# Key features of a batch in one block, its kv products in another, and the selector product in the kv bank

## Chip, cores, metric

One core of a Trainium2 chip. The metric is device time of one execution in microseconds (us). Every run quoted here is of the fast state; the granted TensorE clock (the share of full speed that the throttle left, as a mean of the run) was 0.985 to 1.000. Profiles are of single executions, and their span is some 2.2 us shorter than the time.

## The reference, cut to what matters

Attention with polynomial features, then a feed-forward layer with ELU; 4 batches, 4 heads, 1088 positions, head size 32, rank 8, hidden size 2048.

```python
def phi(x):                                    # 64 features of a row
    a = einsum('rd,bhsd->bhsr', S1, x); b = einsum('rd,bhsd->bhsr', S2, x)
    return einsum('bhsi,bhsj->bhsij', a, b).reshape(..., 64)
kv = einsum('bhsf,bhsd->bhfd', phi(k), v);  z = phi(k).sum(axis=2)
x  = (phi(q) @ kv) / (phi(q) @ z + 1e-6)       # then heads side by side: 4352 x 128
h  = x @ w_in
out = where(h > 0, h, exp(min(h, 0)) - 1) @ w_out
```

All of a batch's keys must have gone into `kv` and `z` before the batch's first query is finished.

## The kernel before

The dense part is a loop of 72 steps. A step multiplies 512 rows by two slices of `w_in` (tile `h`), applies the ELU on ScalarE (`e`: two activations per slice) and VectorE (`gg`), and two steps later adds the product with `w_out` to `o`. `o` has one buffer; when a group (or, for groups 0 and 1, a segment of one) ends, it is emptied into `oT` or `ob` before the next `o` product may start. The attention work of later batches and groups is hung into these steps, between `h` and `o`:

```python
for n in range(N + 4):
    if 2 <= n < N: mm1(g, cp)                     # h: two products of 512 columns
    for f, *a in extra.get(n, ()): f(*a)          # "at": side work, ahead of the ELU
    if 2 <= n < N: elu(g, cp)                     # e on ScalarE, gg on VectorE
    for f, *a in extra.get((n, 1), ()): f(*a)     # "late": after the ELU
    if 2 <= n < N + 2: mm2(...)                   # o of step n - 2; fin1 empties o
```

The side work of one batch, in the order of its data:

```python
KG = [range(0, 4), range(4, 8), range(8, KT)]    # 9 key tiles; the last has 64 rows
def KF(b, gi):                                   # key features: 8, 8 and 1 products
    abp = psum.tile([P, 512], F32, name="abp", tag="aux")     # tag aux: 2 buffers
    for j, i in enumerate(tiles):
        for u in range(rows // 64):
            nc.tensor.matmul(abp[64*u:64*u+64, j*64:j*64+64], kT[b][:, u*KT+i, :], Sab, tile_position=(0, 64*u))
    nc.scalar.copy(ab, abp)                      # ScalarE empties the bank
def KO(b, gi): ...                               # VectorE: kp = outer product of ab
def KA(b, gi): ...                               # kv += kp' v: 16, 16 and 4 products, 64-column tiles
def KC(b): ...                                   # ScalarE: kvz = copy of kv
def KZ1(b): ...                                  # GpSimd: zm = z times a mask
def KZ2(b):                                      # selector product, full width
    wps = psum.tile([P, 512], F32, name="wps", tag="aux")
    nc.tensor.matmul(wps[:, :H*R], SX, zm)
...
for b in range(1, B):
    n = NP * (b * NT // 8) - 12 + 2 * (b == 1)   # 6, 20, 36
    at(n, transp, kT, "k", b, 0, NT)             # VectorE, 1.3 us
    for i in range(3):
        at(n+1+i, KF, b, i); at(n+1+i, KO, b, i); at(n+2+i, KA, b, i)
    late(n+4, KC, b); late(n+4, KZ1, b); late(n+4, KS, b)
    at(n+5, KZ2, b); at(n+3, transp, qT, "q", b, 0, NT)
for g in range(2, NQ):                           # a group's queries
    n = NP * (g - 1) + (g == 2)
    at(n+3, q1, g); late(n+3, q2, g); at(n+5, q4, g); at(n+6, q5, g)
```

`q1` writes `abwp` (query features, 64-column tiles), `q4` writes `qtp` (transposes, full width), `q5` writes `xps` (32-column tiles). Products in float32 appear as two passes each in the trace, transposes as one.

## Time and profile before

| | before |
|---|---|
| time, median of 3 (range) | 303.12 us (302.90 to 303.38) |
| span of the profile | 300.9 us |
| TensorE, ScalarE, VectorE busy | 96%, 62%, 56% |
| dense block, start to start | 1.72 us |

A timeline line gives the start, the duration, the engine, the line of the program, the operation, the tiles (out<-in), the shape, how many passes were merged, and in brackets the idle time before it with what ended it. Durations of matmuls overlap, so what a block costs is the next block's start minus its own. The prediction below shows the lines.

### The profile page before, as it was taken

Reading aid. Unit: us, or ns where it says so; the run is one execution under the profiler, and the core shown is the slowest. Engines: PE = TensorE matmul, PEld = TensorE weight load, DVE = VectorE, ACT = ScalarE, POOL = GpSimd, SP = SyncE. Lnnn points to the kernel's source line nnn. Section 1 sums busy time; section 2 is a strip of 40 time slices with the busy share of each in tenths; the row PEclk is TensorE's granted clock in tenths of the full one; section 3 lists DMA queues with packets and bytes.
Section 4 is the critical chain, followed back from the end, with each engine's and each line's share of the span. In section 5 each row is a group of like instructions: output and inputs, shape, how many; then the busy total and the mean of one; then the engine's idle time right before and its main releaser. Section 6 shows DMA issues by size and latency. Waiting matters only on the chain.

```text
span 300.9 us, 4049 instructions
## 1 busy us (share of the span) xinstructions
PE 290.1 (96%) x1454; PEld 147.7 (49%) x1454; DVE 169.7 (56%) x297; ACT 187.8 (62%) x354; POOL 17.1 (6%) x45
## 2 busy tenths in 40 slices
PE   8987999999999999999999999999999999999994
PEld 5863344644444455444544464445444444444682
DVE  5788899963745565536344656426443644354441
ACT  1526896565666645746775656656774687568682
POOL 2010023440000000100000000100000000000000
PEclk9999999999999999999999999999999999999999
DMA  6932998320010100001001100001001000110020
GB/s 187 338 118 74 200 216 201 48 74 0 9 28 9 27 2 0 2 9 27 2 1 17 18 2 0 0 14 23 0 0 23 16 0 1 15 22 0 3 33 17
DMA packets 38291, 13.37 MB, mean 44 GB/s; under 512 B 32768, under 2 KB 36480, under 8 KB 38272
## 3 DMA queue, kind: packets, MB, share of 16 engines
q1 hardware_dynamic: 37984, 12.86, 19.0%
q10 hardware_dynamic: 288, 0.26, 0.3%
q8 instruction: 11, 0.18, 0.2%
q14 instruction: 8, 0.07, 0.1%
HBM read 10.88 MB, written 2.23 MB: 44 GB/s over the span
## 4 chain that ended last, share of the span: by engine, by line
PE 83%; DVE 8%; ACT 3%; DMA 2%; issue 2%; SPq 1%; DVEq 0%
PE o L522 36%; PE h L493 34%; PE xps L472 3%; PE kv L293 3%; PE qtp L457 2%; PE abwp L360 2%; DMA v<-in_v_dram 2%; DVE gg L508 1%; ACT e L502 1%; PE abp L266 1%; ACT e L501 1%; DVE kT L247 1%; DVE kp L253 1%; DVE W L114 1%; PE x0ps L424 1%
## 5 line engine op out<-in xcount | busy, mean ns | idle before, releaser
L508 DVE SCALAR_TENSOR_TENSOR gg<-e,h 128x512 f32<-128x512 f32 (+1 forms) x144 | 93.0, 654 | 98.3 <-ACT e L502 97.8
L522 PE MATMUL o<-gg,W 128*128 128x512 f32 (+1 forms) x288 | 131.1, 578 | 1.2 <-ACT oT L535 0.7
L493 PE MATMUL h<-xg,W 128*128 128x512 f32 (+1 forms) x288 | 128.8, 569 | 1.8 <-DVE xg L484 0.7
L501 ACT ACTIVATE e<-h 128x512 f32<-128x512 f32 (+1 forms) x144 | 81.4, 565 | 26.1 <-PE h L493 25.7
L502 ACT ACTIVATE e<-e 128x512 f32<-128x512 f32 (+1 forms) x144 | 87.3, 606 | 4.6
L493 PEld LDWEIGHTS h<-xg,W 128*128 128x128 f32 x288 | 54.5, 190 | 65.2 <-issue 55.2
L522 PEld LDWEIGHTS o<-gg,W 128*128 128x128 f32 x288 | 51.9, 190 | 51.4 <-issue 43.7
L270 ACT COPY ab<-abp 128x256 f32<-128x256 f32 (+1 forms) x12 | 3.7, 317 | 25.0 <-PE abp L266 25.0
L365 ACT COPY abw<-abwp 128x384 f32<-128x384 f32 (+1 forms) x8 | 3.7, 458 | 22.9 <-PE abwp L360 22.9
L253 DVE TENSOR_TENSOR kp<-ab 128x1024 f32<-128x1024 f32 (+1 forms) x12 | 12.2, 1022 | 8.4 <-ACT ab L270 8.2
L458 ACT COPY qpT<-qtp 128x512 f32<-128x512 f32 (+1 forms) x16 | 8.3, 561 | 12.6 <-PE qtp L457 12.6
L293 PEld LDWEIGHTS kv<-v,kp 128*64 128x64 f32 (+1 forms) x288 | 9.5, 139 | 7.5 <-DVE gg L508 5.3
L293 PE MATMUL kv<-v,kp 128*64 128x33 f32 (+3 forms) x288 | 10.8, 226 | 0.3 <-DMA v<-in_v_dram 0.3
L381 DVE TENSOR_TENSOR qp<-an,abw 128x1024 f32<-128x1024 f32 (+1 forms) x8 | 9.3, 1159 | 0.3
L472 PE MATMUL xps<-qpT,kvS 64*32 64x128 f32 (+2 forms) x200 | 8.7, 298 | 0.3 <-ACT qpT L458 0.3
L483 ACT COPY xg<-xps 128x256 f32<-128x256 f32 (+1 forms) x8 | 2.9, 359 | 9.8 <-PE xps L472 9.8
L457 PEld LDWEIGHTS qtp<-ident,qp 128*128 128x128 f32 x60 | 6.8, 140 | 4.4 <-issue 4.0
L457 PE MATMUL qtp<-ident,qp 128*128 128x128 f32 x60 | 8.2, 277 | 0.6 <-DVE qp L381 0.6
L313 POOL TENSOR_TENSOR zm<-kvz,zmask 128x32 f32<-128x32 f32 x3 | 0.7, 241 | 126.0 <-ACT kvz L307 126.0
L266 PE MATMUL abp<-Sab,kT 128*64 128x64 f32 x136 | 7.4, 249 | 0.5 <-DVE kT L247 0.5
L360 PEld LDWEIGHTS abwp<-SW,qT 128*64 128x64 f32 x120 | 5.2, 136 | 5.4 <-issue 5.3
L266 PEld LDWEIGHTS abp<-Sab,kT 128*64 128x64 f32 x136 | 6.1, 159 | 3.6 <-issue 2.9
(84 smaller groups left out, 126.2 us busy)
## 6 DMA issues: line engine op xcount, KB each, us to landing
raw<-in_moe_w_in_dram SPq DMA_DIRECT2D x8, 256.0 KB, 5.7
raw<-in_moe_w_out_dram SPq DMA_DIRECT2D x8, 256.0 KB, 6.6
out_dram<-ob SPq DMA_DIRECT2D x104, 16.0 KB, 1.5
hd_k<-in_k_dram SPq DMA_DIRECT2D x3, 544.0 KB, 5.3
hd_q<-in_q_dram SPq DMA_DIRECT2D x3, 544.0 KB, 3.8
v<-in_v_dram SPq DMA_DIRECT2D x12, 72.0 KB, 5.3
v<-in_v_dram SPq DMA_DIRECT2D x12, 64.0 KB, 3.4
hd_k<-in_k_dram SPq DMA_DIRECT2D x1, 288.0 KB, 3.4
```

Of the source, the lines that this page charges most:

```text
L253: nc.vector.tensor_mul(dst, _ap(a_, list(a_.ap[1:]) + [[0, R]]), _ap(b_, [b_.ap[1], [0, R], b_.ap[2]]))
L266: nc.tensor.matmul(abp[64 * u:64 * u + 64, j * 64:j * 64 + 64], kT[b][:, u * KT + i, :], Sab[:].rearrange("p h y -> p (h y)"), skip_group_ ...
L293: nc.tensor.matmul(kv[64 * hp:64 * hp + 64, g2, :n], kp[:rows, j, h].rearrange("p i j -> p (i j)"), _ap(vt[b][:rows, off:off + D], [[VN - ...
L360: nc.tensor.matmul(p[64 * u:64 * u + 64, i * 96:i * 96 + 96], qT[b][:, t, :], SW[:, b].rearrange("p h x r -> p (h x r)"), skip_group_check ...
L381: nc.vector.tensor_mul(qp[g][:, :m], _ap(a_, list(a_.ap[1:]) + [[0, R]]), _ap(b_, [b_.ap[1], [0, R], b_.ap[2]]))
L457: nc.tensor.transpose(p[:, o:o + P], qp[g][:, r:r + 2].rearrange("p t i j -> p (t i j)"), ident[:])
L472: nc.tensor.matmul(xp[w][D * h:D * h + D, :nh * P].rearrange("p (m s) -> p m s", s=P)[:, m0:m0 + m, s], kvS[64 * w:64 * w + 64, b, h, :], ...
L493: nc.tensor.matmul(hs[g, cp][c][:, :n], W[:, cp, c * P:c * P + P], xg[g][:, :n])
L501: nc.scalar.activation(e, hs[g, cp][c][:, :n], RELU, scale=-1.0)
L502: nc.scalar.activation(e, e, EXP, scale=-1.0)
L508: nc.vector.scalar_tensor_tensor(gs[g, cp][:, c, :n], es[g, cp][:, c, :n], -1.0, hs[g, cp][c][:, :n], op0=ADD, op1=MAX)
L522: nc.tensor.matmul(ops[g][:, :n], W[:, cp, (2 + c) * P:(3 + c) * P], gg[:, c, :n], start=(first and c == 0), stop=(last and c == 1))
```

## The change

The intent is to leave the full-width products (128x128 tiles) less often; one such departure to narrower tiles and back is called an excursion below. Key features of a batch stand in one block, the kv products in one block (for batches 2 and 3 next to a group's query features), and the selector product goes into spare columns of the kv bank, so that no third auxiliary buffer is needed near it. The last key product (tile 8, "product 17") shares the bank of the second four tiles.

```diff
     def KF(b, gi):
-        abp = psum.tile([P, 512], F32, name="abp", tag="aux")
+        if gi < 2:
+            abps[b] = psum.tile([P, 512], F32, name="abp", tag="aux")
+        abp = abps[b] if gi < 2 else abps[b][:, 256:]
...
-            kv_ps[b] = psum.tile([P, 2, 2 * D], F32, name="kv", tag="kv", bufs=1)
+            kv_ps[b] = psum.tile([P, 4, 2 * D], F32, name="kv", tag="kv", bufs=1)
...
-        wps = psum.tile([P, 512], F32, name="wps", tag="aux")
+        wps = kv_ps[b][:, 2]
...
-        n = NP * (b * NT // 8) - 12 + 2 * (b == 1)
-        at(n, transp, kT, "k", b, 0, NT)
+        n = NP - 2 if b == 1 else NP * (b * NT // 8 - 2) + 1          # 6, 17, 33
+        at(n - 1, transp, kT, "k", b, 0, NT)
         for i in range(3):
-            at(n + 1 + i, KF, b, i)
-            at(n + 1 + i, KO, b, i)
-            at(n + 2 + i, KA, b, i)
-        late(n + 4, KC, b)          # KZ1, KS alike
-        at(n + 5, KZ2, b)
+            at(n, KF, b, i)
+            at(n + (i > 0), KO, b, i)
+            at(n + 2, KA, b, i)
+        late(n + 2, KC, b)          # KZ1, KS alike
+        at(n + 4, KZ2, b)
```

More of the change, by code (lines that the diff above doesn't have):

```diff
@@ L256 @@
     kvS = const.tile([P, B, H, D], F32, name="kvS")
-    kv_ps, feats, zms, kvz = {}, {}, {}, {}
+    abps, kv_ps, feats, zms, kvz = {}, {}, {}, {}, {}
     def KF(b, gi):
-        abp = psum.tile([P, 512], F32, name="abp", tag="aux")
+        if gi < 2:
+            abps[b] = psum.tile([P, 512], F32, name="abp", tag="aux")
+        abp = abps[b] if gi < 2 else abps[b][:, 256:]
         tiles = KG[gi]
@@ L299, in KC @@
     def KC(b):
-        kv = kv_ps[b][:, :, :D + 1]
+        kv = kv_ps[b][:, :2, :D + 1]
         kvz[b] = work.tile([P, 2, 2, D + 1], F32, name="kvz", tag="kvz")
@@ L630 @@
     for b in range(1, B):
-        n = NP * (b * NT // 8) - 12 + 2 * (b == 1)
-        at(n, transp, kT, "k", b, 0, NT)
+        n = NP - 2 if b == 1 else NP * (b * NT // 8 - 2) + 1
+        at(n - 1, transp, kT, "k", b, 0, NT)
         for i in range(3):
-            at(n + 1 + i, KF, b, i)
-            at(n + 1 + i, KO, b, i)
-            at(n + 2 + i, KA, b, i)
-        late(n + 4, KC, b)
-        late(n + 4, KZ1, b)
-        late(n + 4, KS, b)
-        at(n + 5, KZ2, b)
+            at(n, KF, b, i)
+            at(n + (i > 0), KO, b, i)
+            at(n + 2, KA, b, i)
+        late(n + 2, KC, b)
+        late(n + 2, KZ1, b)
+        late(n + 2, KS, b)
+        at(n + 4, KZ2, b)
         at(n + 3, transp, qT, "q", b, 0, NT)
```

## The prediction

> **What bounds the kernel now.** I read the shares of the page first, then the chain that ended last, then the TensorE timeline of the main part, and only then who waits for whom. The page (busy us, share of the span, instructions; then shares of the chain):
>
> ```profile
> PE 290.1 (96%) x1454; PEld 147.7 (49%) x1454; DVE 169.7 (56%) x297; ACT 187.8 (62%) x354; POOL 17.1 (6%) x45
> ...
> PE 83%; DVE 8%; ACT 3%; DMA 2%; issue 2%; SPq 1%; DVEq 0%
> ```
>
> TensorE is busy nearly always, and the chain runs through it; most of the rest is the first 30 us, where the engines take turns. So time is saved in the main part only by shortening what TensorE issues between two starts. The timeline of TensorE (start, duration, what, how many passes) shows that; durations overlap, so I take differences of starts. Batch 1:
>
> ```profile
> 44.87 1.88 PE L522 MATMUL o<-gg,W 128*128 128x512 f32 x4
> 46.59 1.88 PE L493 MATMUL h<-xg,W 128*128 128x512 f32 x4
> 48.41 0.69 PE L266 MATMUL abp<-Sab,kT 128*64 128x64 f32 x16
> 49.03 1.98 PE L522 MATMUL o<-gg,W 128*128 128x512 f32 x4
> 50.85 1.88 PE L493 MATMUL h<-xg,W 128*128 128x512 f32 x4
> 52.66 1.13 PE L293 MATMUL kv<-v,kp 128*64 128x33 f32 x32
> 53.61 0.66 PE L266 MATMUL abp<-Sab,kT 128*64 128x64 f32 x16
> 54.21 1.98 PE L522 MATMUL o<-gg,W 128*128 128x512 f32 x4
> ...
> 58.79 0.31 PE L266 MATMUL abp<-Sab,kT 128*64 128x64 f32 x2
> ...
> 62.66 0.42 PE L293 MATMUL kv<-v,kp 64*64 64x33 f32 x8
> 63.61 1.98 PE L522 MATMUL o<-gg,W 128*128 128x512 f32 x4 [0.53 <-DVE oT L531]
> ```
>
> A dense block (four passes of 512 columns) costs 1.72 us from start to start (44.87 to 46.59). The h block ahead of a narrow block costs 1.82 (46.59 to 48.41), and the o block after it 1.82 (49.03 to 50.85): an excursion to narrow tiles costs about 0.10 + 0.10 us beside its own passes. A full-width side block pays less: before the transposes at 141.67 the h block took 1.72. The last line shows another loss: 0.53 us in which TensorE waits for VectorE to empty the one "o" buffer.
>
> **What the Trainium skill says.** "Perfetto Trace Analysis", Identifying the Most-Contended Engine, warns that matmul busy share does not measure the distance to roofline. It applies: that is why I use start differences and not the 96%. "TensorEngine Tiling (Array Packing)", Key Properties: "Changing tiling mode (not just tile) drains the TensorE". The 1.72 against 1.82 agrees, at about 0.1 us each way. "PSUM — Partial Sum Buffer", PSUM bank collisions raise a hardware error: its rule is to guard by bank and quadrant, not by address, so two users of different columns of one bank must still be ordered. That bears on the change, since key tiles 4 to 7 and 8 now share one bank. No run here shows a collision; what the ordering costs is estimated below.
>
> **The change, part by part.** No arithmetic is added or removed, so savings are excursions, waits and buffers. The order of the built program shows for each of the batches 1 to 3: 17 key feature products in one block (before 8, 8 and 1); 36 kv products in one block (before 16, 16 and 4), for batches 2 and 3 directly followed by a group's query features; the selector product beside the transposes for batches 2 and 3; the xps block alone. The excess over dense blocks, first before:
> - Batch 1, from 46.59 to 69.09: 22.50 us with ten dense blocks of 1.717, so excess 5.33.
> - Batch 2, from 94.77 to 128.64: 33.87 us with 15 dense blocks (25.75), so excess 8.12. Its parts: query features 0.81, key features 0.61, transposes 1.03, kv 0.95, key features 0.60, xps 1.13, kv 0.95, key feature 0.24, kv 0.35, selector 0.14, and 1.31 of switches and of one wait for kT (the h block at 104.36 took 2.15, of which 0.33 is that wait). Batch 3 repeats this.
>
> The xps block of 1.13 is itself inflated: group 7's, alone at 243.43, takes 0.60. Why, shows in the timeline of all engines:
>
> ```profile
> 113.23 1.20 PE L472 MATMUL xps<-qpT,kvS 64*32 64x256 f32 x16
> 113.34 0.37 ACT L270 COPY ab<-abp 128x256 f32<-128x256 f32 x1 [2.10 <-PE abp L266]
> ...
> 113.77 0.18 PEld L472 LDWEIGHTS xps<-qpT,kvS 64*32 64x32 f32 x14 [0.41 <-ACT ab L270]
> ```
>
> Its second tile waits for the buffer that the key features held. The change separates the two blocks, so this 0.53 goes.
>
> After, by the same rows:
> - Key block of 17. A key product adds (0.60 - 0.24) / 7 = 0.051 us. With its block starting at 0: eight products; the first copy at 0.72 (as 48.41 to the copy at 49.13), the second copy at 0.72 + 8 x 0.051 = 1.13, ending at 1.50. The built program makes product 17 wait for exactly that second copy, because it writes the same bank: it starts near 1.56, and costs 0.24 as the one at 58.79 did. Block 1.80 (without this wait it would be 1.13 to 1.3), with switches **2.00**.
> - kv block: 0.95 + 0.95 + 0.35 = 2.25. Batch 1 alone with switches 2.45; batches 2 and 3 with the query features (0.78) 3.23.
> - Selector: 0.22 in batch 1 as before; with the transposes 0.14 + 0.96 = 1.10.
> - xps alone: 0.60 + 0.20 = 0.80.
>
> Batch 1: 2.00 + 2.45 + 0.22 = 4.67 against 5.33, gain **0.66** (its 0.53 wait for oT counted as gone: the key work that delayed VectorE in that step has moved). Batches 2 and 3: 2.00 + 3.23 + 1.10 + 0.80 = 7.13 against 8.12, gain **0.99** each; the kT wait goes too, as the transpose comes a step ahead and clear of the group's vector work.
>
> Two losses come back. **First, the o buffer.** For batches 2 and 3 the key block now falls into steps 17 and 33, where a group ends and VectorE must empty "o" before the next group's first output product. Before (step 17):
>
> ```profile
> 90.67 0.60 ACT L501 ACTIVATE e<-h 128x512 f32<-128x512 f32 x1 [1.03 <-PE h L493]
> ...
> 93.72 0.68 DVE L531 TENSOR_TENSOR oT<-oT,o 128x512 f32<-128x512 f32 x1
> ...
> 94.77 1.02 PE L522 MATMUL o<-gg,W 128*128 128x512 f32 x2
> ```
>
> The exponentials of the step start 1.06 after its h block (89.61), the buffer is empty at 94.40, and TensorE wants it at 94.77: slack 0.37. In ScalarE's order the three key copies now precede these exponentials. They start 3.82 after the h block (1.81 for that, 1.56 to product 17, 0.35 to its copy, 0.10), so 2.76 later; TensorE is delayed 2.00. Slack 0.37 - 0.76: a new wait near **0.4** per batch. In step 33 the transpose out of "o" ends at 161.12 for a product at 161.45, slack 0.33, same result. **Second, the start:** batch 0's product 17 also waits now, before kv products that already waited 0.33 for v by DMA; I allow **0.2**.
>
> Sum: 0.66 + 2 x (0.99 - 0.42) - 0.2 = 1.6 us.
>
> **The rivals.** (a) Only the drains count and no wait appears: without the wait inside the key block (0.55 each), the o wait and the start loss, 1.6 + 1.65 + 0.84 + 0.2 = 4.3 us, about 298.8. For it: every dense block shows the drains cleanly. Against it: the built program has the wait, and product 17 cannot start before a copy of 0.37. (b) The bunched copies and vector products let ScalarE or VectorE become the bound for some steps, so h buffers are not freed in time. For it: three copies ahead of 2.4 us of exponentials in a step of some 5.4, and in batch 1 the weight rounding shares VectorE, which was busy nearly without a break from 52 to 65. Against it: ScalarE sat 2.5 us idle ahead of the first key copy, and h runs two steps deep. It would eat the gain, about 303. (c) The saved time is hidden elsewhere anyway: spoken against by TensorE's 83% of the chain.
>
> **Range and chances.** Predicted time 303.12 - 1.6, rounded to **301.4** us as the start loss may be hidden. The terms I chose rather than read (product 17's wait, the o wait, the start) can each move it by half a us to one; 8 in 10 between **300.1** and **302.6**. Faster by over 2% would need 297.1, below even rival (a): chance 0.02. Within 2%: 0.97. Slower by over 2%: 0.01.
>
> **What would show it right or wrong.** In the profile after: one key block per batch with a gap near 0.4 to 0.5 charged to the ScalarE copy "ab", three times; kv blocks of 72 passes in about 2.25; xps blocks of 256 columns at 0.60 and no wait of theirs for "ab"; kT waits gone; after the key blocks of batches 2 and 3 an o block waiting about 0.4 for oT and for ob; no such wait near step 10. Wrong if the h blocks wait for gg after the key block (rival b), if product 17 starts without a gap (rival a), or if the first 20 us stretch by more than half a us.

## The result, and the profile after

| | before | after |
|---|---|---|
| median of 4 runs (range) | 303.25 us (302.90 to 303.38) | 302.11 us (301.68 to 302.32) |
| span of the profile | 300.9 us | 299.4 us |

The ratio is 0.9962, interval [0.9945, 0.998]: the same within 2%, with a small gain of about 1.1 us. A ratio here is the mean time of one kernel's fast runs over that of the other's of the same rounds, so not quite the ratio of the medians quoted.

The page of the changed kernel, busy time and chain:

```profile
PE 286.4 (96%) x1454; PEld 146.1 (49%) x1454; DVE 168.9 (56%) x297; ACT 188.1 (63%) x354; POOL 18.5 (6%) x45
...
PE 91%; DVE 4%; ACT 3%; issue 1%; DVEq 0%
```

The same number of passes now takes 3.7 us less busy time (1.7 of it ahead of the first dense o block, near 30 us: there four passes of warm-up products, which the change does not touch, take 2.07 us in the profile before and 1.13 in this one, which is a matter of the run, see the last experiment), and more of the chain lies on TensorE. The TensorE timeline of the changed kernel, batch 1:

```profile
42.66 1.88 PE L496 MATMUL h<-xg,W 128*128 128x512 f32 x4
44.47 1.15 PE L269 MATMUL abp<-Sab,kT 128*64 128x64 f32 x32
46.10 0.33 PE L269 MATMUL abp<-Sab,kT 128*64 128x64 f32 x2 [0.47 <-ACT ab L273]
46.35 1.98 PE L525 MATMUL o<-gg,W 128*128 128x512 f32 x4
...
53.42 2.41 PE L296 MATMUL kv<-v,kp 128*64 128x33 f32 x72
55.76 1.98 PE L525 MATMUL o<-gg,W 128*128 128x512 f32 x4
```

Four narrow excursions became two. Product 17 (46.10) waits 0.47 us for a ScalarE copy. The key block costs 46.35 - 44.47 = 1.88 us, the kv block 2.34. Batch 2 in the same timeline:

```profile
94.16 1.88 PE L496 MATMUL h<-xg,W 128*128 128x512 f32 x4
96.33 1.98 PE L525 MATMUL o<-gg,W 128*128 128x512 f32 x4 [0.28 <-DVE oT L534]
98.15 1.88 PE L496 MATMUL h<-xg,W 128*128 128x512 f32 x4
99.96 2.41 PE L296 MATMUL kv<-v,kp 128*64 128x33 f32 x72
102.30 0.88 PE L363 MATMUL abwp<-SW,qT 128*64 128x96 f32 x16
...
114.66 0.66 PE L475 MATMUL xps<-qpT,kvS 64*32 64x256 f32 x16
115.25 1.98 PE L525 MATMUL o<-gg,W 128*128 128x512 f32 x4
```

The xps block of 1.13 us now takes 0.59. But a new wait stands ahead of the o block at 96.33: the h block before it costs 2.17 in place of 1.72, and the o block 1.82, although no narrow block touches either. In batch 3 it is 2.20 and 1.82. All engines around it:

```profile
91.19 0.84 ACT L273 COPY ab<-abp 128x256 f32<-128x256 f32 x2 [2.51 <-PE abp L269]
...
92.56 0.59 ACT L504 ACTIVATE e<-h 128x512 f32<-128x512 f32 x1
...
95.59 0.68 DVE L534 TENSOR_TENSOR oT<-oT,o 128x512 f32<-128x512 f32 x1
```

The exponentials of this step start at 92.56, 3.91 us after its h block (88.65) where they started 1.06 after it before, because the key copies stand ahead of them. So VectorE empties `o` only at 96.27, and TensorE has been ready since about 95.88 (94.16 + 1.72).

The account by starts, excess over dense blocks of 1.717 us (ten dense blocks on both sides for batch 1; batches 2 and 3, fifteen before and twelve after, counted to the end of the xps block's o block or, before, of the selector's):

| | before | after | gain | predicted |
|---|---|---|---|---|
| batch 1 | 5.33 | 4.87 | 0.46 | 0.66 |
| batch 2 | 8.12 | 7.82 | 0.30 | 0.57 |
| batch 3 | 8.14 | 7.85 | 0.29 | 0.57 |
| until the o block that waits for the first copy of `o` | 37.90 | 37.41 | 0.49 | -0.2 |

The first three make 1.05 us, the whole 1.54, as the spans do (1.5). The runs show 1.1; the last row turned out to be mostly scatter of the start (below).

### The profile page after: what moved, and what is told of

Its sections match the earlier page's. It is cut to its first block, busy times and chain, and to the rows that moved or that the text cites. A ratio compares the mean times of both kernels' runs of the same rounds, so it can differ in the third digit from the quotient of the medians.

```text
span 299.4 us, 4046 instructions
## 1 busy us (share of the span) xinstructions
PE 286.4 (96%) x1454; PEld 146.1 (49%) x1454; DVE 168.9 (56%) x297; ACT 188.1 (63%) x354; POOL 18.5 (6%) x45
## 4 chain that ended last, share of the span: by engine, by line
PE 91%; DVE 4%; ACT 3%; issue 1%; DVEq 0%
PE o L525 39%; PE h L496 37%; PE kv L296 3%; PE xps L475 2%; PE qtp L460 2%; PE abwp L363 2%; PE abp L269 2%; PE idle L216 1%; ACT e L505 1%; ACT e L504 1%; ACT ab L273 1%; PE x0ps L427 1%; DVE kT L247 0%; DVE qp L384 0%; DVE kp L253 0%
## 5 line engine op out<-in xcount | busy, mean ns | idle before, releaser
L253 DVE TENSOR_TENSOR kp<-ab 128x1024 f32<-128x1024 f32 (+1 forms) x12 | 11.0, 943 | 5.0 <-ACT ab L273 5.0
L296 PE MATMUL kv<-v,kp 128*64 128x33 f32 (+3 forms) x288 | 9.9, 224 | 1.0 <-DVE qp L253 1.0
L269 PE MATMUL abp<-Sab,kT 128*64 128x64 f32 x136 | 6.4, 227 | 2.1 <-ACT ab L273 1.9
L106 ACT ACTIVATE W<-W,ebias 128x512 uint32<-128x512 uint32 (+1 forms) x9 | 5.9, 669 | 3.6 <-DVE W L101 3.6
L475 PE MATMUL xps<-qpT,kvS 64*32 64x128 f32 (+2 forms) x200 | 7.6, 298 | 0.3 <-ACT qpT L461 0.3
L269 PEld LDWEIGHTS abp<-Sab,kT 128*64 128x64 f32 x136 | 5.1, 137 | 5.4 <-ACT ab L273 2.4
```

The source lines that it names most:

```text
L253: nc.vector.tensor_mul(dst, _ap(a_, list(a_.ap[1:]) + [[0, R]]), _ap(b_, [b_.ap[1], [0, R], b_.ap[2]]))
L269: nc.tensor.matmul(abp[64 * u:64 * u + 64, j * 64:j * 64 + 64], kT[b][:, u * KT + i, :], Sab[:].rearrange("p h y -> p (h y)"), skip_group_ ...
L296: nc.tensor.matmul(kv[64 * hp:64 * hp + 64, g2, :n], kp[:rows, j, h].rearrange("p i j -> p (i j)"), _ap(vt[b][:rows, off:off + D], [[VN - ...
L475: nc.tensor.matmul(xp[w][D * h:D * h + D, :nh * P].rearrange("p (m s) -> p m s", s=P)[:, m0:m0 + m, s], kvS[64 * w:64 * w + 64, b, h, :], ...
```

## The experiments

All gave right results. They ran in three sets, each with its own runs of the kernel before. The changed kernel itself was run again in the second set alone (e9), so e1 to e4 are compared with it across sets, in which the kernel before has medians of 302.68 to 303.25.

| run | median us (range) | before, same set | ratio [95%] |
|---|---|---|---|
| e1_products_first | 301.02 (301.00 to 304.15) | 302.98 | 0.9957 [0.9923, 0.9991] |
| e2_keys_earlier | 300.92 (300.79 to 302.31) | 302.98 | 0.9938 [0.9918, 0.9958] |
| e3_both | 299.84 (299.42 to 300.20) | 302.98 | 0.9894 [0.9874, 0.9914] |
| e4_copies_late | 299.64 (299.25 to 299.73) | 302.98 | 0.9885 [0.9866, 0.9905] |
| e5_kv_split | 302.65 (302.48 to 302.88) | 303.03 | 0.9973 [0.9933, 1.0012] |
| e6_narrow16 | 309.43 (309.10 to 310.43) | 303.03 | 1.0203 [1.0160, 1.0246] |
| e7_wide16 | 306.13 (305.44 to 308.28) | 303.03 | 1.0094 [1.0051, 1.0137] |
| e9_after_again | 302.23 (302.01 to 303.41) | 303.03 | 0.9962 [0.9924, 1.0000] |
| e10_qT_later | 298.56 (298.51 to 298.78) | 302.68 | 0.9852 [0.9812, 0.9891] |
| e4_again | 299.71 (299.09 to 300.48) | 302.68 | 0.9889 [0.9853, 0.9926] |
| e8_before_selector | 302.96 (302.68 to 303.33) | 302.68 | 0.9999 [0.9958, 1.0039] |

Single executions in all three sets are up to 3 us longer at a lower granted clock (304.15 at 0.988, 308.28 at 0.987, the kernel before 305.69 at 0.985) and pull means and intervals, so sizes are read from medians and from starts in the traces.

### What an excursion costs: e6_narrow16 and e7_wide16

The theory was that leaving the full-width tile mode costs about 0.2 us. The two runs measure it by itself, on the changed kernel:

```diff
+    def extra_mm():
+        p = psum.tile([P, 512], F32, name="xx", tag="aux")
+        nc.tensor.matmul(p[:64, :64], some[:, :64], some[:, :64], tile_position=(0, 0))   # e7: p[:128], some[:, :128], no position
+    for n in (24, 26, 28, 39, 40, 42, 44, 47, 48, 50, 52, 55, 56, 58, 60, 63):
+        at(n, extra_mm)
```

> The change with one extra product of 64 columns through a tile of 64 columns (all 128 rows, two passes, result unused) in each of 16 steps that hold no side work. Theory: each costs 0.24 for its passes and 0.2 for leaving and entering the full-width mode, 0.44 x 16 = 7.0 us slower than the change. Rival (no fixed cost, only the passes): 0.05 to 0.1 each, under 2 us.

> The same 16 extra products, but through the full-width 128x128 tile, 64 columns, two passes. Theory (what is dear is the change of tile mode): like the selector product, 0.14 to 0.17 and at most 0.1 on the o block after it, 0.25 x 16 = 4 us slower than the change, about 3 us less than the narrow ones. Rival (any short block costs the same, whatever its mode): equal to the narrow ones within 0.5 us.

TensorE timeline of e6_narrow16, one of the sixteen:

```profile
120.75 1.88 PE L496 MATMUL h<-xg,W 128*128 128x512 f32 x4
122.56 0.33 PE L655 MATMUL xx<-some 128*64 128x64 f32 x2
122.82 1.98 PE L525 MATMUL o<-gg,W 128*128 128x512 f32 x4
124.64 1.88 PE L496 MATMUL h<-xg,W 128*128 128x512 f32 x4
```

The same of e7_wide16:

```profile
120.73 1.88 PE L496 MATMUL h<-xg,W 128*128 128x512 f32 x4
122.44 0.33 PE L655 MATMUL xx<-some 128*128 128x64 f32 x2
122.61 1.94 PE L525 MATMUL o<-gg,W 128*128 128x512 f32 x4
124.39 1.88 PE L496 MATMUL h<-xg,W 128*128 128x512 f32 x4
```

Narrow: h block 1.81, two passes 0.26, o block 1.82, so 0.46 us in all; 16 make 7.4, and the run is 7.2 slower than the changed kernel in the same set (309.43 against 302.23). Wide: 1.71, 0.17 and 1.78, so 0.23; 16 make 3.7, measured 3.9. For the same columns, half of what the narrow block costs is the change of tile mode: 0.10 before it, 0.09 in it, 0.04 after it. (Beside the mode the two differ in their stationary columns, 64 and 128; a change of mode at equal columns, inside the kv block below, costs 0.10.) The rival (any short block costs the same) falls, and so does the rival of no fixed cost. One thing the theory had not said: this full-width block of two passes too costs the o block after it 0.06. Not every full-width block does: after the eight transposes at 110.22 of the changed kernel the o block costs 1.72 (111.13 to 112.85).

### One more excursion: e5_kv_split

```diff
-            at(n + 2, KA, b, i)
+            at(n + 2 + (i > 0), KA, b, i)
-        late(n + 2, KC, b)          # KZ1, KS alike
+        late(n + 3, KC, b)
```

> The change, but the 36 kv products of a batch in two blocks of 16 and 20 in neighbouring steps: one more excursion per batch, the same products. Theory (an excursion costs about 0.2 us): each of three batches gains one h block of 1.81 in place of 1.72 and one o block of 1.82 in place of 1.72, so 0.6 us slower than the change, ratio to before near 0.998. Rival (only the waits matter): within 0.2 us of the change.

302.65 against 302.23 for the changed kernel in the same set: 0.4 slower by medians; by starts 0.29, 0.20 and 0.19, so 0.7. The direction and size agree with the excursion cost within the scatter. It also shows a misreading: the 16 kv products cost 0.95 when another block of the same mode follows, but 1.05 when the o block follows. Record by record the 0.10 is one step: neighbouring passes of this block start at most 0.07 us apart, and the o block starts 0.15 after the last of them.

### Product 17 ahead of its neighbours' copy: e1_products_first

In the built program product 17 waits for the count that ScalarE reaches with the copy of tiles 4 to 7; the two share one bank. The edit issues it before that copy:

```diff
-        ab = work.tile(...); nc.scalar.copy(ab, abp...); feats[b, gi] = ab, rows
+        if gi != 1:
+            for gj in range(1 if gi else 0, gi + 1):
+                KFC(b, gj)               # the copy; tiles 4 to 7 and 8 both after product 17
```

> The change, but product 17 of each batch is issued ahead of the copy that it shares a bank with (first 4 products and copy, then 5 products, then the two copies). Theory (the ordered bank costs TensorE 0.47 us per batch plus the restart): key blocks of 34 passes in about 1.3 us from start to start and no wait for the ScalarE copy ab; 0.58 x 3 saved, of which about 0.2 in each of batches 2 and 3 goes into a longer wait for the o buffer (0.28 and 0.32 idle now, about 0.5 then), so some 1.3 us faster than the change, about 2.4 faster than before, ratio near 0.992. Rival (that wait hides something that would be waited for anyway): the key block stays near 1.9 us and the time within 0.3 us of the change, ratio near 0.996.

The key blocks take 1.19 us in place of 1.88, without a wait, so the rival falls. But the time fell by 1.1 to 1.2 us against the changed kernel's 302.1 to 302.2, not by the 2.1 that three times 0.69 make. Two places took it back. In batches 2 and 3 the o wait grew (the h block ahead of it to 2.43 and 2.46), as expected, here batch 2 with VectorE's line before it:

```profile
95.37 0.68 DVE L542 TENSOR_TENSOR oT<-oT,o 128x512 f32<-128x512 f32 x1
...
96.10 1.12 PE L533 MATMUL o<-gg,W 128*128 128x512 f32 x2 [0.56 <-DVE oT L542]
```

In batch 1 a wait appeared that nobody had expected: the o block of step 10 waits 0.50 us for oT, and batch 1's excess is 4.84 in place of 4.87. There the whole saving vanished.

### Keys out of the step that empties o: e2_keys_earlier

```diff
-        at(n - 1, transp, kT, "k", b, 0, NT)
+        nk = n - (b > 1)                 # 6, 16, 32; the kv products stay at n + 2
+        at(nk - 1, transp, kT, "k", b, 0, NT)
         for i in range(3):
-            at(n, KF, b, i); at(n + (i > 0), KO, b, i)
+            at(nk, KF, b, i); at(nk + (i > 0), KO, b, i)
```

> The change, but the key block of batches 2 and 3 (with its transpose and first vector product) one step ahead, so that it no longer falls into the step in which a group's o buffer is emptied. Theory (the coincidence makes the o wait): no wait of the o blocks for oT or ob in those steps, h blocks there 1.72 in place of 2.17 and 2.20 and the o blocks after them 1.72 in place of 1.82, so 1.1 us faster than the change, 2.2 faster than before, ratio near 0.993; the waits of product 17 stay at 0.47. Rival (the o buffer is late because of VectorE's load over several steps): the wait turns up again in the same or the next o block and the time stays within 0.3 us of the change.

300.92 us, 2.1 faster than before and 1.2 faster than the changed kernel. The blocks in question, batch 2:

```profile
94.58 1.88 PE L496 MATMUL h<-xg,W 128*128 128x512 f32 x4
96.30 1.88 PE L525 MATMUL o<-gg,W 128*128 128x512 f32 x4
98.02 1.45 PE L496 MATMUL h<-xg,W 128*128 128x512 f32 x3
```

Both cost 1.72, no wait is left, and it did not turn up elsewhere; the waits of product 17 stayed at 0.47. The coincidence with the emptying of `o` made the new wait.

### Both, and the order on ScalarE: e3_both, e4_copies_late, e4_again

e3 joins the edits of e1 and e2. e4 has products first and leaves the key block in steps 17 and 33, but puts the three copies behind that step's exponentials:

```diff
+            if b > 1:
+                late(n, KFC, b, i)
-            at(n + (i > 0), KO, b, i)
+            at(n + (i > 0 or b > 1), KO, b, i)
```

> Both edits: products first, and the key block a step ahead. Theory: the two losses add up without meeting each other, 0.58 x 3 + 1.1 = 2.8 us faster than the change, 3.9 faster than before, ratio near 0.987, near 299.2 us. Rival: they share a cause, and the sum is no more than the better one alone (2.2 to 2.4 faster than before).

> The change with products first, keys of batches 2 and 3 in their step 17 and 33 as in the change, but their three ScalarE copies after that step's exponentials (and the first vector product a step later). Theory (ScalarE's order, copies ahead of exponentials, is what makes the o buffer late): no wait for oT or ob though the key block stands in the same step, time as with both edits, ratio near 0.987. Rival (the mere presence of the key block in that step does it): the o wait stays at 0.3 to 0.6 us, ratio near 0.992.

e3 took 299.84 and e4 299.64 us; neither reached the expected 2.8 us under the changed kernel (2.3 and 2.5 by medians), because batch 1 still gave its part back at step 10. In e4 no o block of batches 2 and 3 waits, though the key block stands in the same step: moving the three copies, and the first key outer product with them, was enough. No run separates the two, but the trace of the changed kernel speaks for the copies: they stood between h and the exponentials (3.91 us above), and VectorE had ended that outer product at 92.83 and then stood idle for 1.02 us, waiting for ScalarE, before the late gg at 93.84. In e3 the o blocks still cost 1.76 and 1.79, a small rest.

> The run with products first and copies late again, as the measure for the one beside it: 299.6 us, with the wait for oT of 0.5 us near 63 us and no wait for oT or ob near 95 and 160 us.

299.71 us, with the same waits: 0.51 for oT in step 10 and none in batches 2 and 3.

### The wait in step 10: e10_qT_later

VectorE in e4, around step 10 (start, duration, line, what):

```profile
60.33 1.32 DVE L247 STREAM_TRANSPOSE qT<-hd_q 128x1088 f32<-128x1088 f32 x1
61.55 1.25 DVE L522 SCALAR_TENSOR_TENSOR gg<-e,h 128x512 f32<-128x512 f32 x2
62.72 0.68 DVE L545 TENSOR_TENSOR oT<-oT,o 128x512 f32<-128x512 f32 x1
...
63.46 1.98 PE L536 MATMUL o<-gg,W 128*128 128x512 f32 x4 [0.51 <-DVE oT L545]
```

The same addition in the changed kernel:

```profile
62.13 0.69 DVE L534 TENSOR_TENSOR oT<-oT,o 128x512 f32<-128x512 f32 x1
```

In e4 TensorE wanted the buffer at about 62.8 and got it at 63.46, 0.06 us after the addition ended (63.40). In the changed kernel the addition ended at 62.82 and the o block started at 62.88. That is the same 0.06 as in the plain waits (96.27 to 96.33 in batch 2), so there was no slack left, and whatever made TensorE earlier there was lost. The transpose of batch 1's queries is not needed before step 12. On top of e4:

```diff
-        at(n + 3, transp, qT, "q", b, 0, NT)
+        at(n + 3 + (b == 1), transp, qT, "q", b, 0, NT)
```

> Products first and copies late, and in addition the transpose of batch 1's queries (1.3 us of VectorE) one step later, step 10 in place of 9. Theory (with products first, batch 1 loses its gain of 0.6 us again at step 10, where VectorE empties o late, after that transpose): no wait for oT near 63 us, the selector block 0.14 in place of 0.81, the output block after it about as before, so 0.65 us faster than the run beside it without this edit, near 299.0 us. Rival (VectorE is the bound through all of steps 5 to 10, with the weight rounding): the wait only shrinks to the next place, and the time stays within 0.2 us of that run.

VectorE in e10:

```profile
60.06 1.36 DVE L522 SCALAR_TENSOR_TENSOR gg<-e,h 128x512 f32<-128x512 f32 x2
61.34 0.68 DVE L545 TENSOR_TENSOR oT<-oT,o 128x512 f32<-128x512 f32 x1
62.73 0.19 DVE L335 TENSOR_TENSOR SW<-kv,bmask 128x32 f32<-128x32 f32 x1 [0.71 <-PE kv L334]
62.84 1.32 DVE L247 STREAM_TRANSPOSE qT<-hd_q 128x1088 f32<-128x1088 f32 x1
```

The addition to `oT` starts 0.67 us after the h block of its step (60.67) where it started 1.79 after it in e4 (60.93), VectorE even waits for TensorE, and the selector block costs 0.14 in place of 0.81. The time is 298.56 us, 1.15 under e4_again, more than the 0.65 expected; the traces give 0.7 for this place and 0.2 for the start, and the rest is scatter between runs. This version beats both kernels: 298.56 us against 302.68, ratio 0.9852, an interval below 1 but a gain under 2%.

### The third part alone, and the start: e8_before_selector and e9_after_again

e8 is the kernel before with nothing but the selector product in the kv bank; e9 is the changed kernel, unedited.

```diff
-            kv_ps[b] = psum.tile([P, 2, 2 * D], F32, name="kv", tag="kv", bufs=1)
+            kv_ps[b] = psum.tile([P, 4, 2 * D], F32, name="kv", tag="kv", bufs=1)
-        kv = kv_ps[b][:, :, :D + 1]
+        kv = kv_ps[b][:, :2, :D + 1]
-        wps = psum.tile([P, 512], F32, name="wps", tag="aux")
+        wps = kv_ps[b][:, 2]
```

> The kernel before with only the third part of the change: the selector product into the kv bank in place of an auxiliary buffer. Theory (auxiliary buffers are not waited for at the selector's place): no change, within 0.3 us of before, ratio 0.999 to 1.001. Rival (it frees a buffer that others wait for): up to 0.5 us faster.

Ratio 0.9999, medians 302.96 and 302.68: no effect by itself, as expected, within an interval of 0.4% each way.

> The changed kernel again, for its time and its first 30 us on this chip. Theory (the earlier first output block in its first profile, 37.41 against 37.90 before, is the state of the start-up, a matter of the run): ratio again near 0.996, and the output block that waits for the first copy of o between 37.2 and 38.0. Rival (the change itself makes the start shorter): always near 37.4.

Ratio 0.9962 again. The o block that waits for the first copy stood at 39.12 in this profile, outside the range expected. The granted clock was 0.50 from 11 to 14 us of it; there the first transposes take 1.97 us from start to end where the first profile of the same kernel has 1.09. The kv products ahead of them waited 1.39 for `v`. In the other profiles with the changed start (e2, e5, e6, e7) the o block stood at 37.62 to 37.85, and in e8, with the start of before, at 37.72. The pace of the first 10 us is a matter of the run as well: the four passes of warm-up products near 4.7 us take 2.07 us in the first profile before and 1.16 in e8, and with the changed start 1.13 in the first profile and 2.08 in e2. So the 0.49 us between the first two profiles are mostly the run; a tenth or two by the change is not excluded.

## Why the prediction was right

**What bounds it.** Right. Every saving that survived is one of TensorE's start differences, and rival (c) falls: e10 is 4.1 us faster than before by medians.

**Excursions.** Right: 0.2 us read from the dense blocks around them, 0.23 measured by itself as the cost of the mode over a full-width block (e6 against e7).

**Product 17.** Right in mechanism, 0.47 in each batch; the key block measured 1.88, estimated 1.80. The 0.051 us per key product was mis-sized, being the difference of two rows with different neighbours: inside the block products start 0.058 apart, so the second copy ends 1.57 us after the block's start in place of 1.50, and product 17 starts at 1.63 in place of 1.56.

**The kv block.** Sized 2.25, measured 2.34. The sum left out a change of mode inside the joined block, whose last four products use 64-row tiles. In batch 2 neighbouring products start 0.06 us apart, but the first 64-row one (101.95) starts 0.16 after the last 128-row one (101.79), so 0.10 more, as at the end of e5's first block. Before, the 16 products ahead were followed by key products in their own mode, so their row did not hold it.

**xps and kT.** Right: 0.59 alone in place of 1.13, and the kT waits of the main part are gone.

**The o wait of batches 2 and 3.** Right in place, cause and size (0.45 and 0.48 by starts, estimated 0.42), but the term missed that the o block after a wait is itself 0.10 longer, and the 0.06 us from the end of VectorE's addition to TensorE's start, which it had counted as slack.

**Step 10.** Right that the wait for oT goes, but with nothing to spare: the o block starts 0.06 us after the addition, as it does when it waits. The prediction had worked out no slack here, so this was luck; e1, e3 and e4 brought the wait back.

**The start.** The loss of 0.2 was not seen. Product 17 of batch 0 does wait 0.46, but the kv products after it then still wait another 0.97 us in the first profile (1.39 in e9, there charged to the load of `v`). The term is smaller than what the start varies by between profiles of the changed start (37.41 to 37.85, without e9), so whether the loss is there stays open.

**The sum.** In the main part predicted 1.80, measured 1.05. The difference is 0.20 in batch 1 and 0.27 and 0.28 in the other two: 0.08 and 0.09 from the key and the kv block each time, and 0.13 and 0.16 from the o wait in batches 2 and 3; a few hundredths either way lie in the selector and query blocks. The large terms lie on the same side, as each was read from rows with other neighbours. The predicted 301.4 us stands against 302.11, inside the range; that it is no further off owes 0.2 to luck: the start's loss, which was counted and not seen.

**Rivals.** Rival (a), 4.3 us without the waits, is what e10 reaches once they are taken away: by starts 1.18 in batch 1, 1.54 and 1.56 in the others, together 4.3. That the sums agree so closely is partly chance: the waits were worth 3.2 us by starts, not the 2.5 that the prediction gave them, and the rest 1.05, not 1.80. Rival (b) did not occur: no h block waits for gg after a key block. But VectorE's load in batch 1, which it named, is what e1, e3 and e4 met in step 10.

## What to carry to other kernels

When TensorE is busy all the time, look at start differences: blocks in another tile mode cost about 0.2 us beyond their passes here, so join them, but count what the joined block then waits for. Two users of one PSUM bank were ordered here through the engine that empties it, at 0.47 us of waiting per batch; issue all products of a bank before its first copy. Work set ahead of another engine's steady work delays a buffer several operations later: check the slack of single-buffered tiles in the step you move into, and after each fix look for the next wait that was only just hidden.

## What the Trainium skill lacked or had wrong

- "TensorEngine Tiling (Array Packing)", Key Properties, states the drain but no cost. Here: 0.23 us per excursion beyond that of a full-width block of the same columns (0.46 against 0.23), and 0.10 for a change between two narrow modes inside the kv block (64-column tiles of 128 rows, then of 64).
- In none of the pages that I read is a price for the dense block that follows an interruption: it costs 1.78 us after two full-width passes (e7) and 1.82 after a wait (0.28 us idle, batch 2 of the changed kernel), in place of 1.72.
- "PSUM — Partial Sum Buffer", PSUM bank collisions raise a hardware error, gives the rule of ordering by bank but not its price. Here it made a key block of 1.19 us one of 1.88.
